# Turning four of eight score blocks off TensorE, and moving sums to GpSimd, in a fused attention and two-layer kernel

## The chip, the cores and the metric

One core of one Trainium2 chip. The metric is the device time of one execution in microseconds, as the median of repeated runs.

## The reference, cut to what matters

The kernel computes chunked attention with memory (4 batches, 8 heads, 768 positions, head size 64; chunks of 32 queries see 8 memory keys, 16 to the left, 8 to the right), then, on 3072 tokens of 512 features, a gated product layer (1536 wide), then a layer with softmax-linear units and a layer norm (1024 wide), all in float32:

```
scores = scale * q_c @ k_full.T ; a = softmax(scores) ; out = a @ v_full
x = ((x @ w_a) * (x @ w_b)) @ w_out
h = x @ w_in ; solu = h * softmax(h)
out = (layernorm(solu) * g_ln) @ w_out2
```

## The kernel before

TensorE multiplies in a reduced float format, so each operand is split in a high part (`[:, 0]`, made by ScalarE as a cast) and a low part (made by VectorE as the difference), and each product is three matmuls. The 3072 tokens are six blocks of 512. Blocks 0 and 1 go through the first layer directly (`ab`, `gate`, `x2_step`); blocks 2 to 5 go through it as two super blocks (`sb` 0 and 1) of two blocks each, with seven products instead of eight per 2x2 of submatrices. Those need sums and differences of the weights, which are made while block 1 is computed: for each of the 12 column groups q of the weights, `s1_whole` adds the high and low part back together into one half of the tile Z (half q % 2), `s1_sums` makes four sums in it, `s1_hi` casts them, `s1_lo` makes the low part in place, and both are stored to DRAM (`ws`). `wo_keep` stores the third weight and, for seven of twelve, a sum of its parts. During super block 0 `wo_load`, `wo_sums`, `wo_hi`, `wo_lo` and `wo_store` do the like for w_out in six parts p, and `piece_load` brings pieces of it into slot 8 for `third_mm`.

Attention for the later blocks is computed while the first layer of an earlier one runs. A "pair" d is two query groups of 128 queries. Pairs d0 to d0 + 3 (blocks 2 and 3) run inside block 1, pairs d0 + 4 to d0 + 7 inside super block 0. A pair has the steps `pair_P` (mask), `pair_S` (128 score matmuls), `pair_M` (maximum, subtract), `pair_X` (exponential into the tile EB), `pair_N` (sum, reciprocal, product in EB), `pair_T` (eight 128x128 transposes on TensorE into PSUM, and a copy back to EB on ScalarE), and `pair_V` (128 value matmuls, and a copy to the tile `xst`). The tiles X0 and X1 (`xst`) collect the results of blocks 2 and 3; `x1_hi`, `x1_lo` and `t1_sum` make operands of them.

The order on TensorE, VectorE, ScalarE and, from block 1 on, SyncE's DMA queue is the order in which the program is written. A clock of "ticks" lays it out: `at(t, fn, ...)` puts a step behind tick t, and `tick()` is called after each group of matmuls. Block 1 has 12 column groups f with six ticks of six matmuls each: two for the first product, two for the second (then `gate`, which multiplies and casts), two for `x2_step` of f - 1 (with `gate_lo` before its second tick). So ticks 0 to 71 are block 1, and super block 0 follows. `when(0, f, k)` gives a tick of super block 0. Loads of q, k and v for pairs go through `pair_load(d, i, values)` into three buffers in turn (`ld_tile`). GpSimd's order is not written out by hand; it makes few sums before the last stage. The pairs' places (P, S, M, X, N, T, V in ticks), the s1 steps' places and the first loads of w_out's pieces, all six ahead of super block 0:

```
pair(d0 + j, [16 * j + k for k in (-2 if j else 0, 0, 1, 2, 3, 8, 10)])
for k, fn in zip(places, (s1_whole, s1_sums, s1_hi, s1_lo)):
    at(16 * (q // 3) + k, fn, q)
for p in range(HF):
    piece_load(p)
```

Of the kernel before, what the change touches and what calls it, by code (L numbers as in the profile page):

```python
# [55 lines left out]
def fused_kernel(  # L56
# [24 lines left out]
    wos = [dram.tile([P, 4, 2, 256], F32, name=f"wos{p}") for p in range(HF)]  # L81
    ztd = [dram.tile([P // 32, P // 32, 32, NF2 * 32], F32, name=f"ztd{i}") for i in range(4)]
# [4 lines left out]
    ld_p = ctx.enter_context(tc.tile_pool(name="ld", bufs=3))  # L87

    def ld_tile(n, name):
        return ld_p.tile([P, n], F32, tag="ld", name=name, padded_shape=[P, NP * (GQ + GK)])  # L90
# [42 lines left out]

    turn = {}

    def next_of(name, n):

        turn[name] = (turn.get(name, -1) + 1) % n
        return turn[name]
# [154 lines left out]
    def pair_load(d, i, values):  # L294

        qi = 2 * d + i
        n = NP * (GQ + GK) + NCH * NP * D
        q, k = NP * GQ, NP * (GQ + GK)
        if values:
            t = ld_tile(n - k, "v")  # L300
            nc.sync.dma_start(t, qkv[qi, :, k:n])
            quads[qi]["v"] = t.rearrange("k (c p d) -> k c p d", c=NCH, p=NP)
        else:
            t = ld_tile(k, "qk")
# [33 lines left out]

    def pair_X(d):
        e = EB.rearrange("q g (p r k) -> q r (g p) k", p=NP, r=2)  # L340
        nc.scalar.activation(out=e, in_=pairs[d].pop("all"), func=AF.Exp, scale=SCALE)

    def pair_N(d):
        e = EB.rearrange("q g (h k) -> q (g h) k", h=H)
        sm = sm_p.tile([P, 2 * H, 1], F32, tag="sm2", name="sm")
        nc.vector.tensor_reduce(out=sm, in_=e, op=ALU.add, axis=AX.X)
        nc.vector.tensor_scalar_add(sm, sm, 1e-9)
        nc.vector.reciprocal(out=sm, in_=sm)
        nc.vector.tensor_tensor(
            out=e, in0=e, in1=sm.to_broadcast([P, 2 * H, CK]), op=ALU.mult  # L350
        )

    def pair_T(d):
        e = EB.rearrange("q g (p rk) -> q (g p) rk", p=NP)
        pt = ps_at.tile([P, 2 * NP, GQ], F32, tag="at", name="pt")
        for p in range(2 * NP):
            nc.tensor.transpose(pt[:, p, :], e[:, p, :], ident)
        nc.scalar.copy(EB.rearrange("q g (p t) -> q (g p) t", p=NP), pt)
# [11 lines left out]
    def pair_V1(d, i):  # L370
# [3 lines left out]
        at = EB[:, i].rearrange("q (p t) -> q p t", p=NP)  # L374
        for c in range(NCH):
            t = slice(CQ * c, CQ * c + CQ)
            for p in range(NP):
                half = 64 * (p % 2)
                for r in range(2):
# [4 lines left out]
                        at[rows, p, t],  # L384
# [4 lines left out]
    def pair_V2(d):  # L389
        pair_V1(d, 1)  # L390
        full = pairs[d].pop("px")
        bi, off = d // 2, d % 2 * 2 * GQ
        if off == 0:
            xst[bi % 2] = x_tile(bi % 2, F32, "xs")
# [100 lines left out]
    def wo_keep(f):  # L495
# [12 lines left out]
    def s1_whole(q):  # L508
# [3 lines left out]
        nc.vector.tensor_tensor(  # L512
# [63 lines left out]
    def t1_sum(n):  # L576

        a, b = stage(0), stage(1)
        if n == 0:
            xsrc.update(zip((3, 2, 6), (  # L580
                ld_tile(2 * TB, "t").rearrange("d (k t) -> d k t", k=2) for _ in range(3)
# [70 lines left out]
    def wo_sums(p):  # L652
        z = flat(wo_z(p)).rearrange("p (i c) -> p i c", i=4)
        for o, a, b, op in (
# [5 lines left out]
            nc.vector.tensor_tensor(out=z[:, o], in0=z[:, a], in1=z[:, b], op=op)  # L660
# [144 lines left out]
    def w2_raws(n):  # L805
        held.setdefault("ld", []).extend(ld_tile(2 * WC, "w2ld") for _ in range(n))
# [614 lines left out]
    def pair(d, places):  # L1421
        p, s, m, x, n, t, v = places
        for k, fn in zip(places, (pair_P, pair_S, pair_M, pair_X, pair_N, pair_T, pair_V)):
# [5 lines left out]
            if fn is pair_S:  # L1429
                at(k, pair_load, d, 1, True)  # L1430
                if d % 4 < 3:
                    at(k, pair_load, d + 1, 0, False)
            if fn in (pair_V, pair_V2) and d % 4 < 3:
                at(k, pair_load, d + 1, 1, False)
                at(k, pair_load, d + 1, 0, True)
# [498 lines left out]
```

## Time and profile before

| what | us |
|---|---|
| median of three runs | 879.94 (879.82 to 880.74) |
| the profiled execution | 880.53 |
| its span | 878.8 |
| TensorE matmul busy | 858.5 |
| VectorE busy | 718.3 |
| ScalarE busy | 398.0 |
| GpSimd busy | 63.5 |

The span is the time from the first to the last instruction of one profiled execution; the execution's own time has some 1.7 us more around it. Busy times are those of one engine's instructions without overlaps counted twice. The durations of single matmuls overlap, so the time that one takes of TensorE's queue is read from where the next begins.

### The profile page before, as it was taken

What the parts mean: (1) busy time and instruction counts of PE and PEld (TensorE: products, weight loads), DVE (VectorE), ACT (ScalarE), POOL (GpSimd) and SP (SyncE); (2) the same over time, 40 slices, a digit from 0 to 9 for tenths busy, and PEclk for the clock granted to TensorE, in tenths of its full rate; (3) what the DMA queues carried; (4) which work ended last, traced back from release to release, by engine and by line L of the source; (5) the groups of instructions that cost most, each with busy time, mean ns of one, the idle gap of its engine ahead of it and who ended that gap; (6) DMA issues with size and microseconds to landing.
All of it is one profiled execution on the core that took longest, in us unless ns stands there. A gap on an engine that the chain in (4) does not pass through costs nothing.

```text
span 878.8 us, 16702 instructions
## 1 busy us (share of the span) xinstructions
PE 858.5 (98%) x6696; PEld 709.5 (81%) x6696; DVE 718.3 (82%) x1162; ACT 398.0 (45%) x587; POOL 63.5 (7%) x77
## 2 busy tenths in 40 slices
PE   4899999999999999999999999999999999999998
PEld 3788888788888888888888888888888888888887
DVE  6999966978876676777967778998589999999892
ACT  3777633333343323334645544257354444544432
POOL 0000000000000000000000000000322222322110
PEclk9999999999999999999999999999999999999999
DMA  9995447876799878872799988558913545564344
GB/s 370 423 415 218 162 145 230 282 239 211 249 342 412 304 289 343 318 293 89 258 324 337 341 323 324 208 200 288 322 41 97 163 151 179 163 186 128 120 144 133
DMA packets 96254, 214.49 MB, mean 244 GB/s; under 512 B 7728, under 2 KB 58672, under 8 KB 90928
## 3 DMA queue, kind: packets, MB, share of 16 engines
q1 hardware_dynamic: 96144, 213.42, 68.1%
q8 instruction: 53, 0.87, 0.4%
q14 instruction: 25, 0.20, 0.1%
q0 software_dynamic: 32, 0.00, 0.0%
HBM read 147.85 MB, written 65.54 MB: 243 GB/s over the span
## 4 chain that ended last, share of the span: by engine, by line
PE 93%; DVE 3%; ACT 2%; DMA 1%; issue 1%; SPq 0%; ACTq 0%; DVEq 0%
PE acc L784 25%; PE pab L1220 15%; PE acc L998 13%; PE pab L755 7%; PE acc L755 5%; PE pab L885 5%; PE pab L886 5%; PE pab L887 5%; PE acc L885 3%; PE acc L887 2%; PE acc L886 2%; PE px L381 2%; PE s L193 2%; PE px L267 1%; DMA qkv<-qkv_dram 1%
## 5 line engine op out<-in xcount | busy, mean ns | idle before, releaser
L784 PE MATMUL acc<-w 128*128 128x512 f32 x978 | 227.6, 391 | 0.0
L784 PEld LDWEIGHTS acc<-w 128*128 128x128 f32 x978 | 182.6, 188 | 38.4 <-DMA w<-ws 0.3
L1220 PE MATMUL pab<-w 128*128 128x512 f32 (+1 forms) x600 | 134.3, 381 | 0.0
L1220 PEld LDWEIGHTS pab<-w 128*128 128x128 f32 x600 | 109.4, 188 | 21.9 <-DVE w L1197 0.3
L885 PE MATMUL pab<-x,w 128*128 128x512 f32 (+1 forms) x200 | 78.9, 394 | 1.5 <-ACT x L286 0.9
L946 POOL TENSOR_TENSOR w2ld<-w2ld 128x256 f32<-128x256 f32 x44 | 38.9, 906 | 540.5 <-ACT r L775 492.3
L886 PE MATMUL pab<-x,w 128*128 128x512 f32 (+1 forms) x200 | 77.2, 386 | 0.1
L887 PE MATMUL pab<-x,w 128*128 128x512 f32 (+1 forms) x200 | 77.1, 385 | 0.0
L755 PE MATMUL pab<-w 128*128 128x512 f32 x288 | 70.2, 390 | 0.1
L797 DVE TENSOR_TENSOR part<-acc,part 128x512 f32<-128x512 f32 x56 | 38.6, 690 | 33.3 <-PE acc L784 26.5
L755 PEld LDWEIGHTS pab<-w 128*128 128x128 f32 x288 | 53.8, 188 | 11.6 <-ACT w L726 0.5
L998 PE MATMUL acc<-w,hx 128*128 128x512 f32 x252 | 60.6, 390 | 0.1
L998 PE MATMUL acc<-w 128*128 128x512 f32 x252 | 60.3, 390 | 0.0
L998 PEld LDWEIGHTS acc<-w,hx 128*128 128x128 f32 x252 | 47.1, 188 | 10.3 <-DVE mx L1014 0.5
L998 PEld LDWEIGHTS acc<-w 128*128 128x128 f32 x252 | 47.2, 188 | 9.8
L755 PE MATMUL acc<-w 128*128 128x512 f32 x216 | 51.7, 389 | 0.0
L755 PEld LDWEIGHTS acc<-w 128*128 128x128 f32 x216 | 40.5, 188 | 8.4
L885 PEld LDWEIGHTS pab<-x,w 128*128 128x128 f32 x200 | 38.1, 191 | 9.7 <-ACT x L286 1.2
L887 PEld LDWEIGHTS pab<-x,w 128*128 128x128 f32 x200 | 38.2, 191 | 7.5
L886 PEld LDWEIGHTS pab<-x,w 128*128 128x128 f32 x200 | 38.2, 191 | 7.3 <-DVE x L290 0.4
L730 DVE TENSOR_TENSOR w<-r,w 128x512 fp32r<-128x512 f32 x56 | 37.9, 693 | 1.9 <-ACT w L726 1.9
L885 PE MATMUL acc<-gh,w 128*128 128x512 f32 x96 | 38.2, 397 | 0.0
(237 smaller groups left out, 1406.9 us busy)
## 6 DMA issues: line engine op xcount, KB each, us to landing
w<-ws SPq DMA_DIRECT2D x24, 1024.0 KB, 6.8
w<-ws SPq DMA_DIRECT2D x24, 768.0 KB, 6.0
raw<-w1d_dram SPq DMA_DIRECT2D x11, 1536.0 KB, 22.6
qk<-qkv_dram SPq DMA_DIRECT2D x20, 640.0 KB, 6.6
ws<-Z SPq DMA_DIRECT2D x24, 512.0 KB, 4.9
w<-wos SPq DMA_DIRECT2D x48, 256.0 KB, 4.1
ztd<-r SPq DMA_DIRECT2D x84, 128.0 KB, 2.3
v<-qkv_dram SPq DMA_DIRECT2D x20, 512.0 KB, 5.8
```

Source lines behind the costliest of these rows:

```text
L193: nc.tensor.matmul(s[CQ * c:CQ * c + CQ, r, p, lo:hi], st["q"][rows, p, CQ * c:CQ * c + CQ], st["k"][rows, p, k0 + lo:k0 + hi], start=True ...
L381: nc.tensor.matmul(px[half:half + 64, r, p // 2, i, t], v[rows, c, p, :], at[rows, p, t], start=True, stop=True,)
L730: nc.vector.tensor_tensor(out=c[:, 1], in0=op_src(k), in1=c[:, 0].bitcast(F32), op=ALU.subtract)
L755: nc.tensor.matmul(ps, w[:, u, sl], g[:, v], start=first and n == 0, stop=last and n == 2, skip_group_check=True,)
L784: nc.tensor.matmul(ps, w[:, u, k], xx[v][:, k], start=(start and k == 0 and i == 0), stop=(stop and k == 1 and i == 2), skip_group_check=True,
L797: nc.vector.tensor_tensor(out=o, in0=a, in1=b, op=op)
L885: nc.tensor.matmul(ps, wl, xh, start=first, stop=False)
L886: nc.tensor.matmul(ps, wh, xl, start=False, stop=False)
L887: nc.tensor.matmul(ps, wh, xh, start=False, stop=last)
L946: (nc.gpsimd if j else nc.vector).tensor_tensor(out=s4[:, i], in0=a, in1=b, op=op)
L998: nc.tensor.matmul(ps, x, y, start=(start and k == 0 and i == 0), stop=(stop and k == 1 and i == 2), skip_group_check=True,)
L1220: nc.tensor.matmul(po, s[x][:, f], wo2(f)[:, h, sl], start=(m == 0), stop=(m == 3 * NF2 - 1))
```

## The change

For pairs d0 to d0 + 3 the transposes on TensorE go. VectorE turns all of EB (128x1024) in 32x32 squares, four DMAs store it to DRAM (`etd`) so that chunk and key change places, and one DMA loads it into the columns of the X tile where the pair's result will stand later. `pair_X` and `pair_N` order EB by (r, 32-column half, head pair, column) for it, the first as two exponentials, the second with its product in two halves. The value products read the X tile. Their place moves to behind the next pair's scores, and the loads of q, k and v are put in other buffers and places for it. `s1_whole`, the sums of `wo_keep` and `wo_sums` run on GpSimd instead of VectorE, with new places for some s1 steps. The six first pieces of w_out are loaded one per f of super block 0. The core of the diff:

```diff
     def pair_T(d):
+        if not by_dma(d):
...
+            return
+        e = EB.rearrange("q r x -> q (r x)")
+        nc.vector.transpose(out=e, in_=e)
+
+    def pair_O(d):
+        m = etd[d % 2].rearrange("(i k) c x -> k i c x", i=4)
+        for c in range(NCH):
+            nc.sync.dma_start(
+                m[:, :, c], EB[CQ * c:CQ * c + CQ].rearrange("k r (b x) -> k (r b) x", b=2)
+            )
+
+    def pair_R(d):
+        bi, off = pair_xs(d)
+        at = xst[bi % 2][:, :, off:off + 2 * GQ]
+        nc.sync.dma_start(at, etd[d % 2])
+        pairs[d]["at"] = at.rearrange("k c (g p t) -> k c g p t", g=2, p=NP)
...
-                        at[rows, p, t],
+                        at[rows, c, i, p],
...
     def wo_keep(f):
...
-            nc.vector.tensor_tensor(out=t, in0=w[:, 0], in1=w[:, 1], op=ALU.add)
+            nc.gpsimd.tensor_tensor(out=t, in0=w[:, 0], in1=w[:, 1], op=ALU.add)
...
     def s1_whole(q):
...
-        nc.vector.tensor_tensor(
+        nc.gpsimd.tensor_tensor(
             out=s1[q].rearrange("p (a c) -> p a c", a=2), in0=w[:, :, 0], in1=w[:, :, 1],
...
     def wo_sums(p):
...
-            nc.vector.tensor_tensor(out=z[:, o], in0=z[:, a], in1=z[:, b], op=op)
+            nc.gpsimd.tensor_tensor(out=z[:, o], in0=z[:, a], in1=z[:, b], op=op)
...
+            if fn is pair_S and d % 4 == 0:
+                for i in range(2):
+                    at(k + 4, pair_load, d + 1, i, False, i)
+            if fn is pair_S and d % 4:
+                at(k, pair_load, d - 1, 1, True, 0)
+                at(k, pair_load, d, 0, True, d % 2 or 2)
+            if fn is pair_V:
+                if d % 4 < 2:
+                    at(k, pair_load, d + 2, 0, False, 0)
+                    at(k, pair_load, d + 2, 1, False, 1 + (d + 1) % 2)
+                if d % 4 == 2:
+                    at(k, pair_load, d + 1, 1, True, 0)
...
-        pair(d0 + j, [16 * j + k for k in (-2 if j else 0, 0, 1, 2, 3, 8, 10)])
+        pair(d0 + j, [(0, 16, 31, 46)[j] + k for k in (
+            (-2 if j else 0, 0, 1, 2, 4 - (j > 0), 6 - (j > 0) - (j > 2), 7 - 2 * (j > 2), 10 - (j > 2), 17 if j > 2 else 23)
+        )])
...
-        places = ((1, 3, 6, 8), (8, 9, 11, 13), (14, 15, 17, 20))[q % 3]
-        if q == 6:
-            places = 1, 3, 8, 9
+        places = ((0, 3, 6, 8), (7, 9, 11, 13), (13, 15, 17, 20))[q % 3]
+        if q < 4:
+            places = ((2, 7, 8, 10), (9, 11, 14, 16), (14, 17, 19, 20), (1, 5, 7, 8))[q]
...
-        at((0, 0, 14, 14, 14, 32, 32, 44, 48, 52, 56, 60)[f], wo_keep, f)
+        at((0, 0, 18, 19, 20, 34, 35, 44, 48, 52, 56, 60)[f], wo_keep, f)
...
+        at(when(0, p + 1, 1), piece_load, p)
         at(when(1, p, 2), piece_load, p)
...
-    for p in range(HF):
-        piece_load(p)
```

So pair j has its scores behind tick 0, 16, 31 and 46, its turn behind tick 6, 21, 36 and 50, its stores behind 7, 23, 38 and 51, its load behind 10, 26, 41 and 55, and its values behind 23, 39, 54 and 63.

## Rows read from the trace of the kernel before

**Rows 1.** The page: span, busy time of TensorE and VectorE.

```profile
span 878.8 us, 16702 instructions
...
PE   858.5 (98%) x6696; PEld 709.5 (81%) x6696; DVE 718.3 (82%) x1162; ACT 398.0 (45%) x587; POOL 63.5 (7%) x77
```

**Rows 2.** Windows: stretch, length, busy us of each engine, granted clock, DMA share, GB/s.

```profile
147.00:262.00 115.00, 113.86 (x1478) 94.60 (x1479) 95.30 (x136) 42.52 (x54) 0.00 (x0) 0.99 0.77 260
262.00:410.00 148.00, 148.00 (x1624) 121.95 (x1623) 101.61 (x149) 51.92 (x77) 0.00 (x0) 1.00 0.79 299
...
147.00:150.00 3.00, 2.96 (x122) 2.74 (x126) 1.51 (x3) 0.00 (x0) 0.00 (x0) 0.50 0.56 175
```

**Rows 3.** TensorE's timeline: start, us, what, [idle before, releaser]; first and second pair.

```profile
157.74 1.06 PE L357 MATMUL pt<-ident,EB 128*128 128x128 f32 x8 [0.82 <-DVE EB L349]
...
161.84 2.07 PE L381 MATMUL px<-EB,v 64*64 64x32 f32 x128 [0.28 <-ACT EB L358]
...
172.24 1.54 PE L193 MATMUL s<-qk 64*32 64x64 f32 x128
...
184.50 0.39 PE L887 MATMUL pab<-x,w 128*128 128x512 f32 x1
184.74 1.03 PE L357 MATMUL pt<-ident,EB 128*128 128x128 f32 x8
185.53 0.48 PE L885 MATMUL pab<-x,w 128*128 128x512 f32 x1
185.84 0.40 PE L886 MATMUL pab<-x,w 128*128 128x512 f32 x1
```

**Rows 4.** The chain that ended last: one run of 36 matmuls.

```profile
430.84 8.16 PE acc L755 x36
```

**Rows 5.** VectorE's groups by line, 147 to 262 us: busy us, mean ns.

```profile
L526 DVE TENSOR_TENSOR Z<-Z 128x256 f32<-128x256 f32 x48 | 20.4, 424 | 1.3
L543 DVE TENSOR_TENSOR Z<-Z 128x1024 fp32r<-128x1024 f32 x12 | 14.7, 1222 | 3.3 <-ACT Z L536 3.3
L512 DVE TENSOR_TENSOR Z<-w 128x1024 f32<-128x1024 f32 x12 | 14.6, 1217 | 1.9 <-DMA ws<-Z 1.9
...
L900 DVE TENSOR_TENSOR G<-G,pab 128x512 f32<-128x512 f32 x12 | 8.2, 684 | 7.6 <-PE pab L887 7.6
...
L349 DVE TENSOR_TENSOR EB<-EB,sm 128x1024 f32<-128x1024 f32 x4 | 4.9, 1226 | 0.1
...
L503 DVE TENSOR_TENSOR wz<-w 128x512 f32<-128x512 f32 x7 | 4.5, 684 | 0.0
```

**Rows 6.** Groups by line, whole span: GpSimd's sums, wo_sums, VectorE's 32x32 turn.

```profile
L946 POOL TENSOR_TENSOR w2ld<-w2ld 128x256 f32<-128x256 f32 x44 | 38.9, 906 | 540.5 <-ACT r L775 492.3 <-DVE w L975 28.0 <-DVE hx L975 19.4
...
L1169 DVE STREAM_TRANSPOSE r<-r 128x1024 f32<-128x1024 f32 x13 | 16.2, 1244 | 0.2
...
L660 DVE TENSOR_TENSOR r<-r 128x256 f32<-128x256 f32 x24 | 10.2, 424 | 0.6
...
L225 POOL TENSOR_TENSOR EB<-EB,sm 128x512 f32<-128x512 f32 x2 | 2.1, 1044 | 121.9 <-DVE sm L224 121.9
```

**Rows 7.** DMA issues, 147 to 262 us: KB each, median us to landing.

```profile
ws<-Z SPq DMA_DIRECT2D x24, 512.0 KB, 4.9
qk<-qkv_dram SPq DMA_DIRECT2D x6, 640.0 KB, 6.2
v<-qkv_dram SPq DMA_DIRECT2D x7, 512.0 KB, 5.6
```

**Rows 8.** DMA issues of the page, whole span: the last stage's stores.

```profile
ztd<-r SPq DMA_DIRECT2D x84, 128.0 KB, 2.3
```

**Rows 9.** Timelines of VectorE and GpSimd, 660 to 700 us: one meeting.

```profile
691.92 1.72 DVE L1106 TENSOR_TENSOR r<-r,EB 128x1024 f32<-128x1024 f32 x1
...
688.50 4.06 POOL L946 TENSOR_TENSOR w2ld<-w2ld 128x256 f32<-128x256 f32 x4 [4.64 <-DVE hx L975]
```

More of the change, by code (lines that the diff above doesn't have):

```diff
@@ L81, in fused_kernel @@
     wos = [dram.tile([P, 4, 2, 256], F32, name=f"wos{p}") for p in range(HF)]
+    etd = [dram.tile([P, NCH, 8 * CQ], F32, name=f"etd{i}") for i in range(2)]
     ztd = [dram.tile([P // 32, P // 32, 32, NF2 * 32], F32, name=f"ztd{i}") for i in range(4)]
@@ L337, in pair_M, with by_dma @@
         )
+    def by_dma(d):
+        return d < 4 * NDIR
     def pair_X(d):
-        e = EB.rearrange("q g (p r k) -> q r (g p) k", p=NP, r=2)
-        nc.scalar.activation(out=e, in_=pairs[d].pop("all"), func=AF.Exp, scale=SCALE)
-    def pair_N(d):
-        e = EB.rearrange("q g (h k) -> q (g h) k", h=H)
-        sm = sm_p.tile([P, 2 * H, 1], F32, tag="sm2", name="sm")
-        nc.vector.tensor_reduce(out=sm, in_=e, op=ALU.add, axis=AX.X)
+        if not by_dma(d):
+            e = EB.rearrange("q g (p r k) -> q r (g p) k", p=NP, r=2)
+            nc.scalar.activation(out=e, in_=pairs[d].pop("all"), func=AF.Exp, scale=SCALE)
+            return
+        e = EB.rearrange("q r (b n k) -> q r n b k", b=2, n=2 * NP)
+        s = pairs[d].pop("all").rearrange("q r n (b k) -> q r n b k", b=2)
+        for r in range(2):
+            nc.scalar.activation(out=e[:, r], in_=s[:, r], func=AF.Exp, scale=SCALE)
@@ L347, in pair_N @@
         nc.vector.tensor_scalar_add(sm, sm, 1e-9)
         nc.vector.reciprocal(out=sm, in_=sm)
-        nc.vector.tensor_tensor(
-            out=e, in0=e, in1=sm.to_broadcast([P, 2 * H, CK]), op=ALU.mult
-        )
-    def pair_T(d):
[L354 to L358, printed above, removed]
+        for r in range(2):
+            nc.vector.tensor_tensor(
+                out=EB[:, r].rearrange("q (b n k) -> q b n k", b=2, n=2 * NP),
+                in0=EB[:, r].rearrange("q (b n k) -> q b n k", b=2, n=2 * NP),
+                in1=sm[:, r].rearrange("q (b n k) -> q b n k", b=1, k=1).to_broadcast(
+                    [P, 2, 2 * NP, 32]),
+                op=ALU.mult,
+            )
@@ new lines, in pair_T @@
+    def pair_T(d):
+        if not by_dma(d):
+            e = EB.rearrange("q g (p rk) -> q (g p) rk", p=NP)
+            pt = ps_at.tile([P, 2 * NP, GQ], F32, tag="at", name="pt")
+            for p in range(2 * NP):
+                nc.tensor.transpose(pt[:, p, :], e[:, p, :], ident)
+            nc.scalar.copy(EB.rearrange("q g (p t) -> q (g p) t", p=NP), pt)
+            pairs[d]["at"] = EB.rearrange("q g (p c t) -> q c g p t", p=NP, c=NCH)
+            return
+        e = EB.rearrange("q r x -> q (r x)")
+        nc.vector.transpose(out=e, in_=e)
@@ L580, in t1_sum @@
             xsrc.update(zip((3, 2, 6), (
[L581 removed]
+                ld_tile(2 * TB, "t", i).rearrange("d (k t) -> d k t", k=2) for i in range(3)
             )))
@@ L805, in w2_raws @@
     def w2_raws(n):
-        held.setdefault("ld", []).extend(ld_tile(2 * WC, "w2ld") for _ in range(n))
+        t = held.setdefault("ld", [])
+        t += [ld_tile(2 * WC, "w2ld", len(t) + i) for i in range(n)]
     def w2_z(i):
@@ L1508, in fused_kernel @@
     )):
-        pair(d0 + 4 + j, [when(0, f, k) for f, k in places])
-    for t, *n in ((74, 0, False), (74, 1, False), (78, 0, True)):
+        places = [when(0, f, k) for f, k in places]
+        pair(d0 + 4 + j, [*places[:6], None, None, places[6]])
+    for t, *n in ((74, 0, False, 0), (74, 1, False, 1), (78, 0, True, 2)):
         at(t, pair_load, d0 + 4, *n)
```

75 lines of the change are left out of this document (49 added, 26 removed).

## The prediction, made before the run

> **What bounds the kernel now.** I read the page's busy shares first: TensorE is busy 858.5 of 878.8 us, VectorE 718.3 [rows 1]. So TensorE's queue is the kernel, and an edit gains only if it takes instructions or idle time out of that queue. Next the windows by stage. The edits lie in the second block (147 to 262 us) and the first super block after it (262 to 410). TensorE is busy 113.86 of 115 us in the one and all 148 in the other [rows 2]. In the first window 1.14 us of idle time is thus all that could be recovered besides work; in the second nothing. VectorE is busy 95.3 of the 115 us and 101.6 of the 148: heavily loaded, but not what TensorE waits for, since TensorE does not stop.
>
> The reader should then find the idle time in TensorE's timeline. Before the first pair's eight transposes it waits 0.82 us for VectorE's normalised EB, and before that pair's value products 0.28 us for ScalarE's copy of the turned EB [rows 3]. That is 1.10 of the 1.14 us. The second pair's transposes begin with no wait, and so do the third's and fourth's.
>
> **The change part by part.**
>
> *Transposes leave TensorE.* In the timeline a matmul starts at 184.50, the eight transposes at 184.74, the next matmul at 185.53 and the one after at 185.84 [rows 3]. A matmul normally takes 8.16/36 = 0.227 us of the queue [rows 4]. So the eight cost 185.53 - 184.50 - 0.227 = 0.80 us, and the restart 0.31 - 0.227 = 0.08 more: 0.88 us. Four pairs: **3.5 us**. Nothing replaces them on TensorE: scores and value products keep their number and shapes, the value products read 32 contiguous columns as before, only from the X tile instead of EB.
>
> *The two waits.* With values at tick 23 after scores at tick 0, neither the normalisation nor a copy of EB stands before a TensorE instruction: **1.1 us**. If the wait merely moves, this term is 0.
>
> *VectorE.* A 32x32 turn of 128x1024 takes 1.245 us [rows 6], the normalising product in two halves some 0.2 more than its 1.23 [rows 5] (an estimate from the fixed part that 424 ns for 256 columns against 1222 for 1024 imply). Four pairs add 5.7 us. The twelve s1_whole (14.6) and seven wo_keep sums (4.5) leave it [rows 5], in the next stage the 24 wo_sums (10.2) [rows 6]. Net it falls from 95.3 to about 82 us in the block and from 101.6 to 91 behind it. TensorE has no use for that: worth 0. ScalarE loses a copy per pair and splits an exponential, on an engine busy 42.5 of 115 us [rows 2]: 0.
>
> *The way through DRAM.* Four stores of 128 KB per pair; the nearest row is ztd<-r, the same size, 2.3 us to landing [rows 8]. One load of 512 KB; the nearest row is v, 5.6 us [rows 7]. A tick is six matmuls, 1.36 us [rows 4]. Pair 0: store at tick 7, load at 10, values at 23: 13 ticks or 17.7 us for 5.6. The shortest is pair 3: load at 55, values at 63: 10.9 us. Cost 0 while these margins stand. The load waits on SyncE's queue for the stores to land, and everything later on that queue (Z stores, loads of the next q, k and v) waits with it, for at most the 2.3 us.
>
> *Loads of q, k and v change places.* Pair 3's two q,k loads are issued after pair 1's values (tick 39), its scores follow tick 46: 7 ticks, 9.5 us, for two loads of 6.2 us median that start 0.5 us apart and share the DMA engines [rows 7]. I take 7.5 us, so 2 us in hand. Pair 2 has 8 ticks. The DMA share is 0.77 in this stretch [rows 2] and the new way adds 4 MB to its 115 us x 260 GB/s = 30 MB, so there is room on average.
>
> *Sums on GpSimd.* The trace shows 128x512 at 1044 ns and 128x256 at 906 ns on GpSimd [rows 6]. An s1_whole (128x1024) lies between twice the first, 2.1 us, and four times the second, 3.6 us; I take 2.1, its runs of 512 being nearest to the first. It frees VectorE and is due only at s1_sums. The loop for one half of Z is whole 2.1 to 3.6, sums 4 x 0.424 = 1.7, cast and lo 1.2 each [rows 5] (the cast taken as long as lo), store 4.9 [rows 7]: 11.1 to 12.6 us. Two q's have 32/3 ticks, 14.5 us, plus the inserted scores and values. It fits.
>
> The tightest place is q = 10. Count from the start of pair 3's scores. VectorE then has M 2.4, sums(8) 1.7, x1_lo 1.2, N 3.1, turn 1.2, gate 0.7, sums(9) 1.7, gate_lo 0.7, lo(8) 1.2 [rows 5, 6], after 1.54 us of scores [rows 3]: lo(8) ends at 15.4. Its store lands at 20.3, GpSimd ends at 22.4 to 23.9, sums(10) and gate_lo(9) at 24.8 to 26.3. TensorE wants gate_lo(9) behind tick 63, at 17 x 1.36 + 1.54 + 2 x 2.07 = 28.8. So 2.5 to 4 us in hand: cost 0.
>
> There is a row against free overlap of the two engines: a soft_mult of 128x1024 takes 1.72 us where VectorE's other sums and products of that size take 1.22 [rows 5], and it begins at 691.92 while GpSimd runs its h_sums from 688.50 to 692.56 [rows 9]. So a collision costs VectorE about 0.5 us. The Trainium skill, "SBUF — State Buffer", Who interferes with whom, says that a VectorE instruction with two SBUF inputs and a GpSimd instruction reading SBUF lock each other out until the first has finished; the trace agrees with that row. By it each of the 19 sums of this block could hold VectorE for its whole 1.0 to 2.1 us rather than 0.5; at the worst VectorE would get no relief, and the sum above would still be -4.6 us, as TensorE doesn't wait for it.
>
> By the row, 19 collisions are at most 9.5 us of VectorE, half of the 19.1 it is rid of.
>
> *wo_sums and wo's pieces.* Each wo_sums becomes 4 x 906 = 3.6 us instead of 1.7, but GpSimd starts when the load lands: wo_load comes 9 or more ticks (12 us) before its sums' old place. ScalarE's wo_hi, two ticks behind that place, finds them done: 0. The six pieces, loaded one per f and used some 12 ticks later, are as hidden as they were: 0.
>
> **Sum.** 3.5 + 1.1 = 4.6 us. The profiled execution took 880.53 us (its span 878.8 and 1.7 around it), so 875.9 for one like it; the median of the runs is 0.59 below that execution, so **875.3 us**.
>
> **Rivals.**
>
> 1. *A late transfer takes a share.* For it: the margin of 2 us at pair 3's scores, and SyncE's queue now stands behind the turn (store) and behind the store (load). Against: q,k loads with only 4.5 ticks behind the values stop TensorE nowhere now. If pair 2's and 3's loads take 9.5 to 11 us instead of 7.5, each stop costs up to 1.5 us, and a load of pair 3's turned weights another 1: 1 to 4 us, so 876.3 to 879.3.
>
> 2. *VectorE, held by GpSimd, makes TensorE wait: slower.* VectorE's order is fixed, so a late GpSimd sum holds gate_lo behind it, and TensorE's x2 step wants that. It decides from the point where VectorE is over 2.5 to 4 us late at tick 64. Eight collisions of 0.5 us before it, or a store landing at 9 instead of 4.9 us, bring it there. At q = 7, 9 and 10, 2 to 3 us each are 6 to 9 us lost: 877 to 884, taken as 882. Against: the block has net 13 us less for VectorE.
>
> 3. *The wait moves, the work goes.* Only the 3.5 us are won, the 1.1 us come back elsewhere (the first wait for pair 0's turned weights cannot, at 17.7 us): 876.4.
>
> 4. *A bonus.* From 147 to 150 us TensorE has a granted clock of 0.50, its 1.2 GHz level [rows 2], after a stretch of small products and waits at the end of the first block. Those 3 us cost 1.5. The change touches nothing in front of them, but the loads and VectorE's first sums there move; if the fall were gone: 873.8.
>
> **How the numbers follow.** The forecast has 0.58, rival 1 0.16, rival 2 0.10, rival 3 0.11, rival 4 0.05. Forecast's own range: 3.2 (restarts not counted) to 1.14 + 3.6 = 4.7 us, with the runs' own 0.9 us of spread: 874.6 to 876.7. The range of 873.8 to 878.3 leaves out rival 2 and the upper third of rival 1, and the rest is some 8 in 10. A measurement of this kernel can tell about 0.2%, 1.76 us, from no change. Faster: forecast, 3, 4 and two thirds of 1, 0.84, less a little for what I haven't seen: 0.81. Same: the rest of 1 and part of 2: 0.10. Slower: 0.09.
>
> **What the profile after would show.** No transposes out of EB for four of the eight pairs; TensorE's busy time and span down by 3.5 or more; no idle before the first pair's values; the lines of pair_T on VectorE at about 1.25 us, x4; s1_whole on GpSimd at 2.1 us (3.6 would be the other bound); VectorE's waits for GpSimd new, under 3 us each; TensorE's idle time in the second block under 0.3 us. The prediction is wrong if TensorE waits for q,k loads before the third or fourth pair's scores, for X before the values, or for gh or gl at an x2 step.

## The result, and the profile after

The changed kernel takes **890.32 us** (median of four runs, 889.19 to 890.66); the kernel before, run beside it, 880.15 (879.82 to 880.74). The ratio is 1.0113 [1.0095, 1.013]: slower by 1.1%, where 0.5% faster was forecast. One execution of the runs below, the profiled one of loads_first2 (1431.6 us at a granted clock of 0.56 throughout), is in no median and no comparison.

The page after, with the lines that answer to [rows 1]:

```profile
span 888.3 us, 16721 instructions
...
PE 858.1 (97%) x6664; PEld 708.2 (80%) x6664; DVE 705.8 (79%) x1127; ACT 393.5 (44%) x587; POOL 122.8 (14%) x120
```

32 transposes have left TensorE, as the change says. Its busy time is still nearly what it was, and the span is 9.5 us longer: idle time has come in, and TensorE spends more of its time at the lower clock, where a matmul of 512 columns is busy for 0.63 us and not 0.39. The windows after, to be set against [rows 2]; the last two are stretches at the lower clock, 10.2 us in all, where the kernel before has one of 3.4, from 146.95 (the execution's last 1.4 us not counted; busy us of TensorE, its weight loads, VectorE, ScalarE, GpSimd; granted clock, DMA share, GB/s):

```profile
147.00:262.00 115.00, 108.93 (x1491) 90.17 (x1492) 82.96 (x122) 36.52 (x53) 29.62 (x13) 0.96 0.83 273
262.00:410.00 148.00, 145.42 (x1609) 119.04 (x1608) 92.72 (x121) 51.03 (x74) 19.54 (x24) 1.00 0.84 314
...
147.27:154.08 6.81, 5.61 (x180) 4.70 (x183) 0.97 (x3) 1.23 (x3) 0.00 (x0) 0.50 0.39 115
225.78:229.17 3.39, 2.95 (x68) 2.44 (x69) 1.69 (x2) 0.00 (x0) 1.43 (x1) 0.50 1.09 386
```

VectorE has the relief that was worked out (95.3 to 83.0 us in the second block), and TensorE stands still 6.1 of 115 us in place of 1.1. TensorE's timeline names the places; for landmarks it holds the first matmul of the scores of pairs d0, d0 + 4 and d0 + 7:

```profile
142.66 1.14 PE L270 MATMUL px<-AT,v 64*64 64x32 f32 x64
146.88 0.79 PE L238 MATMUL pt<-ident,EB 128*128 128x128 f32 x4 [3.08 <-DVE EB L228]
...
152.63 1.94 PE L196 MATMUL s<-qk 64*32 64x64 f32 x128
...
196.76 1.47 PE L196 MATMUL s<-qk 64*32 64x48 f32 x128 [0.59 <-PE pab L944]
...
224.76 0.85 PE L196 MATMUL s<-qk 64*32 64x64 f32 x64 [3.67 <-DMA qk<-qkv_dram]
226.22 1.19 PE L196 MATMUL s<-qk 64*32 64x64 f32 x64 [0.61 <-DMA qk<-qkv_dram]
...
280.79 1.47 PE L196 MATMUL s<-qk 64*32 64x64 f32 x128
...
284.36 0.96 PE L840 MATMUL acc<-w 128*128 128x512 f32 x3 [1.67 <-issue]
...
380.10 0.32 PE L439 MATMUL px<-EB,v 64*64 64x32 f32 x7 [0.80 <-issue]
...
387.37 1.47 PE L196 MATMUL s<-qk 64*32 64x64 f32 x128
```

The same landmarks before, in its own timeline:

```profile
148.40 2.05 PE L193 MATMUL s<-qk 64*32 64x64 f32 x128
...
275.08 1.47 PE L193 MATMUL s<-qk 64*32 64x64 f32 x128
...
378.38 1.47 PE L193 MATMUL s<-qk 64*32 64x64 f32 x128
```

The reader is to see four things. TensorE is 4.2 us late at the first pair's scores (152.63 against 148.40), before the changed block has begun. It is 5.7 us late at 280.79, 9.0 at 387.37 and 9.5 at the end. None of the idle time of [rows 3] is left. And three of the new stops are not where the prediction looked: the end of the first block, and two stops with no releaser (the waits of an engine that no semaphore in the trace ends; `issue` in the rows). Worked out over the rows: 4.2 to the first landmark; in the second block 0.59 + 3.67 + 0.61 of waits and half of the 3.4 us at 1.2 GHz behind them, 1.7, less the 4.6 that the change takes out, is 2.0 (the landmarks say 1.5); then 1.67 and 0.80. Some 1.3 us to the end I have not placed, but for a gap of 0.29 at 600 us.

### The profile page after: what moved, and what is told of

Same layout as the page of the kernel before. It is cut to its first block, busy times and chain, and to the rows that moved or that the text cites. A ratio compares the mean times of both kernels' runs of the same rounds, so it can differ in the third digit from the quotient of the medians.

```text
span 888.3 us, 16721 instructions
## 1 busy us (share of the span) xinstructions
PE 858.1 (97%) x6664; PEld 708.2 (80%) x6664; DVE 705.8 (79%) x1127; ACT 393.5 (44%) x587; POOL 122.8 (14%) x120
## 4 chain that ended last, share of the span: by engine, by line
PE 86%; DMA 5%; DVE 4%; ACT 2%; issue 2%; SPq 1%; POOL 0%; ACTq 0%; POOLq 0%
PE acc L840 25%; PE pab L1277 13%; PE acc L1055 12%; PE pab L811 7%; PE acc L811 5%; PE pab L942 4%; PE pab L943 4%; PE pab L944 4%; PE acc L942 2%; PE acc L944 2%; PE acc L943 2%; DMA ws<-Z 2%; PE s L196 1%; PE px L270 1%; PE px L439 1%
## 5 line engine op out<-in xcount | busy, mean ns | idle before, releaser
L1055 PEld LDWEIGHTS acc<-w,hx 128*128 128x128 f32 x252 | 47.2, 188 | 10.2 <-DVE mx L1071 0.5
L568 POOL TENSOR_TENSOR Z<-w 128x1024 f32<-128x1024 f32 x12 | 30.5, 2542 | 76.9 <-DMA ws<-Z 65.2
```

Source lines behind the costliest of these rows:

```text
L568: nc.gpsimd.tensor_tensor(out=s1[q].rearrange("p (a c) -> p a c", a=2), in0=w[:, :, 0], in1=w[:, :, 1], op=ALU.add,)
L1055: nc.tensor.matmul(ps, x, y, start=(start and k == 0 and i == 0), stop=(stop and k == 1 and i == 2), skip_group_check=True,)
```

## The experiments

The expectations give their theories letters. **A**: the sums on GpSimd cost the time, first of all where s1_whole of q = 0 and 1 meets VectorE at the end of the first block. **A2** (A in loads_first, F in final1 and final2): SyncE's order costs it, as loads of q, k stand behind stores; against it **B2**: the DMA engines are full there, so that an earlier issue lands no earlier. **B** and **E**: the way through DRAM as a whole is the cause. **C**: the stops with no releaser depend on where instructions lie in TensorE's program, not on what they do. **D**: the loop of store, GpSimd's sum and VectorE's sums over the halves of Z makes VectorE late. "Pair 2" and "pair 3" in them are pairs d0 + 2 and d0 + 3, the third and fourth here. The medians in one table; the kernel before, run beside them, had 880.2 to 880.7:

| run | us | ratio to before [95%] |
|---|---|---|
| sums_vec | 894.66 | 1.0167 [1.015, 1.0184] |
| gp_only | 887.56 | 1.0079 [1.0062, 1.0096] |
| early_vec | 888.45 | 1.0096 [1.0081, 1.0111] |
| gp_early_vec | 883.84 | 1.0039 [1.0025, 1.0052] |
| loads_first | 898.46 | 1.0204 [1.0182, 1.0225] |
| loads_first2 | 892.22 | 1.0148 [1.0119, 1.0176] |
| both | 892.8 | 1.014 [1.0119, 1.016] |
| both_pad | 891.42 | 1.0127 [1.0105, 1.015] |
| loads_act | 890.84 | 1.0134 [1.0111, 1.0156] |
| no_dram | 887.04 | 1.0079 [1.0064, 1.0094] |
| pad_only | 889.7 | 1.0102 [1.0084, 1.012] |
| all3 | 891.09 | 1.012 [1.0105, 1.0135] |
| z3 | 890.83 | 1.012 [1.0096, 1.0145] |
| z3_early_pad | 886.63 | 1.0066 [1.0048, 1.0084] |
| final1 | 888.54 | 1.0109 [1.0088, 1.0131] |
| final2 | 889.5 | 1.0112 [1.0096, 1.0128] |

### GpSimd's sums alone, and the turn alone

sums_vec: the changed kernel with all three sums back on VectorE.

```diff
-            nc.gpsimd.tensor_tensor(out=t, in0=w[:, 0], in1=w[:, 1], op=ALU.add)
+            nc.vector.tensor_tensor(out=t, in0=w[:, 0], in1=w[:, 1], op=ALU.add)
...
-        nc.gpsimd.tensor_tensor(
+        nc.vector.tensor_tensor(
...
-            nc.gpsimd.tensor_tensor(out=z[:, o], in0=z[:, a], in1=z[:, b], op=op)
+            nc.vector.tensor_tensor(out=z[:, o], in0=z[:, a], in1=z[:, b], op=op)
```

> The changed kernel with all three kinds of sums (s1_whole, wo_keep's sums, wo_sums) back on VectorE at the changed places; the turn through DRAM stays. Theory A (GpSimd's sums run free of the ticks: two s1_whole at 141.6 us hold VectorE up before the last transposes of the first block, 3.1 us of TensorE idle and 3.4 us more at 1.2 GHz, and later VectorE waits for them, so that pair 3's q and k are loaded late, 4.3 us of idle and another 3.4 us at 1.2 GHz): the first loss goes (-4.8 us), the second goes or shrinks: 879.5 to 883 us, no idle over 0.5 us before the transposes at 141 us. Rival B (the way through DRAM on SyncE's queue is the cause, GpSimd is not): 888 or more, the wait for q and k at pair 3's scores stays at 4 us.

gp_only: the kernel before with the three sums on GpSimd, and nothing else of the change.

```diff
-            nc.vector.tensor_tensor(out=t, in0=w[:, 0], in1=w[:, 1], op=ALU.add)
+            nc.gpsimd.tensor_tensor(out=t, in0=w[:, 0], in1=w[:, 1], op=ALU.add)
...
```

s1_whole and wo_sums are changed in the same way.

> The kernel before with the three kinds of sums on GpSimd at the places of before, nothing else changed. Theory A: the first loss comes alone, some 3 us idle before the last transposes of the first block and 1.7 us of slow clock, so 884 to 886 us; the pairs' turns by TensorE stay, and VectorE's waits for s1_whole may add 1 to 3 us to it through a late EB. Rival B: 879 to 881 us, as before.

The two parts, the turn with its moved loads and places and the sums, cost 14.3 and 7.2 us by themselves and 10.2 together, so each is a loss, and the sums on GpSimd buy back some of what the turn costs. For sums_vec theory A missed: the stop at 147 is gone, but VectorE, now with the turn on top of all its sums, makes TensorE wait at other places. TensorE's timeline of sums_vec:

```profile
187.33 0.50 PE L942 MATMUL pab<-x,w 128*128 128x512 f32 x1 [3.08 <-DVE G L957]
...
222.79 0.50 PE L943 MATMUL acc<-gh,w 128*128 128x512 f32 x1 [1.22 <-DVE gh L963]
...
228.09 1.17 PE L196 MATMUL s<-qk 64*32 64x64 f32 x64 [3.87 <-ACT gh L959]
```

For gp_only theory A held in its mechanism, though 887.56 us is above its 884 to 886: with no turn, no stores and no moved load, the stop at the end of the first block is there with nearly the same size. TensorE's timeline of gp_only:

```profile
145.63 1.11 PE L235 MATMUL pt<-ident,EB 128*128 128x128 f32 x4 [2.89 <-DVE EB L225]
```

### The meeting at the end of the first block

GpSimd's timeline of the changed kernel, and VectorE's for the same stretch:

```profile
130.56 5.46 POOL L559 TENSOR_TENSOR wz<-w 128x512 f32<-128x512 f32 x4 [3.84 <-PE pab L943]
141.60 4.67 POOL L568 TENSOR_TENSOR Z<-w 128x1024 f32<-128x1024 f32 x2 [5.58 <-ACT EB L217]
```

```profile
138.41 0.17 DVE L226 TENSOR_SCALAR sm<-sm 128x8 f32<-128x8 f32 x1
...
138.86 0.69 DVE L228 TENSOR_TENSOR EB<-EB,sm 128x512 f32<-128x512 f32 x1
...
142.35 1.66 DVE L226 TENSOR_SCALAR sm<-sm 128x8 f32<-128x8 f32 x1
...
144.28 2.55 DVE L228 TENSOR_TENSOR EB<-EB,sm 128x512 f32<-128x512 f32 x1
```

GpSimd has the block's first sums in its queue with nothing ahead of them, and starts when their data are free, at 130 and 141 us; the program has them behind tick 0 and later, and the six matmuls of tick 0 begin at 150.81. VectorE's two last steps of the first block, alone 0.17 and 0.69 us a few us before, take 1.66 and 2.55 beside it, and TensorE's last transposes of that block wait for them. The two additions on GpSimd end at 143.98 and 146.27; the first of the two steps ends at 144.0, the second at 146.8, as if each had waited for the addition beside it. early_vec takes only this meeting away.

```diff
-        nc.gpsimd.tensor_tensor(
+        (nc.vector if q < 2 else nc.gpsimd).tensor_tensor(
```

> The changed kernel with the s1_whole of q = 0 and 1 alone back on VectorE, at their ticks. Theory A: the 3.1 us idle before the transposes of the first block's last queries go, and the slow clock there is as short as before (3.4 us): 890.3 - 4.8 = 885.5 us; pair 3's wait for q and k stays, about 4 us. If the idle time there has another cause: 890.

VectorE's and TensorE's timelines of early_vec:

```profile
141.80 0.69 DVE L228 TENSOR_TENSOR EB<-EB,sm 128x512 f32<-128x512 f32 x1
```

```profile
145.80 0.38 PE L942 MATMUL pab<-x,w 128*128 128x256 f32 x1 [0.48 <-ACT x L289]
...
219.89 1.17 PE L196 MATMUL s<-qk 64*32 64x64 f32 x64 [3.07 <-DMA qk<-qkv_dram]
```

The first matmul behind that block stands at 145.80, in the changed kernel at 150.81: 5.0 us won there, 3.08 of the wait and 1.9 at 1.2 GHz. The time falls by 1.9 only. What is lost again stands in the same timeline: waits of 1.66 before the third pair's scores (0.59 in the changed kernel), 3.07 + 0.60 before the fourth's (3.67 + 0.61), 1.63 and 1.27 with no releaser (1.67 and 0.80), and stretches of 6.8 and 3.4 us at 1.2 GHz behind them, for one of 3.4. In six profiles of kernels that keep the meeting TensorE waits 1.1 to 3.1 us there. In that of loads_act GpSimd starts at 142.80, when VectorE is done with these steps, and it costs nothing; so a microsecond decides it.

gp_early_vec is the same edit on gp_only: no turn, and no early meeting.

> The kernel before with the sums on GpSimd, except the s1_whole of q = 0 and 1: what GpSimd's sums cost without the meeting at the end of the first block. Theory A2: 887.6 - 2.9 (idle) - 3.4 (6.8 us less at 1.2 GHz) = 881.3, of which 1 to 2 are VectorE's later EB; if GpSimd's sums cost elsewhere too: over 883.

It is the best of the runs with sums on GpSimd, and still 3.2 us over before (ten runs from 880.86 to 886.12). GpSimd's other sums thus cost about 3 us by themselves; where, its profile does not show, since that execution was one of the shortest (881.37). It is not the clock: the six executions at a mean granted clock of 1.000 spread from 880.9 to 884.9.

### SyncE's order before the fourth pair's scores

SyncE's timeline of the changed kernel (start, us to issue), and two rows of its DMA issues: q, k issued from 218.0 to 218.5 us, and the load of pair d0 + 2's turned weights (KB, us to landing):

```profile
214.34 0.37 SPq L587 DMA_DIRECT2D ws<-Z  x1
214.75 2.71 SPq L401 DMA_DIRECT2D etd<-EB  x4
...
218.05 1.68 SPq L310 DMA_DIRECT2D qk<-qkv_dram  x2
```

```profile
qk<-qkv_dram SPq DMA_DIRECT2D x1, 640.0 KB, 6.6
...
xs<-etd SPq DMA_DIRECT2D x1, 512.0 KB, 8.5
```

The values of pair d0 + 1 end at 211.3 (209.26 + 2.07), and from then on the loads could go. They go at 218.05 and behind it, 6.7 us later: a store of Z stands ahead of them and waits for VectorE's low part, and four stores behind it take 2.71 us to issue. That low part stands in VectorE's order behind the sums of q = 6 and the turn, and part of its lateness is a wait for GpSimd, whose half of Z waits for a store to land. GpSimd's and VectorE's timelines show it for q = 5:

```profile
197.62 3.14 POOL L568 TENSOR_TENSOR Z<-w 128x1024 f32<-128x1024 f32 x1 [5.91 <-DMA ws<-Z]
```

```profile
200.80 1.80 DVE L582 TENSOR_TENSOR Z<-Z 128x256 f32<-128x256 f32 x4 [2.29 <-POOL Z L568]
...
213.09 1.18 DVE L599 TENSOR_TENSOR Z<-Z 128x1024 fp32r<-128x1024 f32 x1
```

This wait is not all of it: z3 below takes it out, and the loads go only 0.5 us earlier.

Two kernels put the loads ahead of the stores. loads_first moves pair d0 + 2's stores behind its tick 39, and q = 5's last step with them; in it, q = 5's low part is made from a buffer that already holds q = 6's high part.

```diff
-    7 - 2 * (j > 2), 10 - (j > 2)
+    7 + (j == 2) - 2 * (j > 2), 10 - (j > 2)
...
+        if q == 5:
+            places = 13, 15, 17, 23
```

> The changed kernel with two places moved: pair 2's four stores behind the loads of pair 3's q and k on SyncE's queue (tick 39 instead of 38), and q = 5's low part with its store behind them too (tick 39 instead of 36). Theory A: the loads are issued some 6 us earlier, right behind pair 1's values, pair 3's scores wait under 0.5 us and the slow clock behind them is gone: 890.3 - 4.3 - 1.7 = 884.3 us. If the loads were slow because the DMA engines are full, not because they were issued late: 888 to 890, and the loads take over 8 us to land.

loads_first2 moves only the DMAs; in it, q = 5's low part is stored after q = 7's first sum has overwritten that half of Z, and so too in both and both_pad.

```diff
-        s1_store(q, 0, h)
+        if q == 6:
+            at(39, s1_store, q, 0, h)
+        else:
+            s1_store(q, 0, h)
```

The same is done for the low part of q = 5, with loads_first's place of the stores.

> The changed kernel with the order on SyncE's queue changed around tick 39 alone: pair 3's q and k are loaded ahead of pair 2's four stores to DRAM and of two stores of weight sums (q = 5 low, q = 6 high); every engine computes in the order of the changed kernel. Theory A2 (these loads were late because they stood behind stores that waited for a late VectorE): they are issued right behind pair 1's values, some 6 us earlier, and the 4.3 us of idle time before pair 3's scores go with their 3.4 us at 1.2 GHz (1.7 us): 884 to 885 us. Rival B2 (the DMA engines are full there, so issuing earlier doesn't land them earlier): the idle time stays over 2 us, 887 to 890.

Both lost more than they won: 8 and 2 us over the changed kernel. In loads_first the wait before the fourth scores is gone, and 6.00 us for VectorE's gate and 4.04 for the next load of turned weights stand in its place. Its trace shows why: the stores of Z now stand behind the loads, GpSimd waits 18.4 us for one to land before its next sum, and VectorE 10.6 us for that sum. As the moved steps also change what waits for what, neither kernel tests the order alone. There is no trace of loads_first2 to compare; both, which adds early_vec's edit to it, shows the same in TensorE's timeline:

> That order on SyncE's queue, and the s1_whole of q = 0 and 1 on VectorE. Theory A2: the two losses are separate places and add: 890.3 - 5.0 - 6.0 = 879.3 us, with idle time left only where nothing in the profile is waited for (some 3 us in all). If one loss merely moves: 883 or more.

```profile
241.09 0.50 PE L948 MATMUL pab<-x,w 128*128 128x512 f32 x1 [2.81 <-DVE G L963]
...
254.86 2.25 PE L439 MATMUL px<-xs,v 64*64 64x32 f32 x128 [2.60 <-DMA xs<-etd]
```

loads_act issues these loads from ScalarE's queue instead, so that nothing of SyncE's stands ahead:

```diff
-                    at(k, pair_load, d + 2, 0, False, 0)
-                    at(k, pair_load, d + 2, 1, False, 1 + (d + 1) % 2)
+                    at(k, pair_load, d + 2, 0, False, 0, nc.scalar)
+                    at(k, pair_load, d + 2, 1, False, 1 + (d + 1) % 2, nc.scalar)
```

> The changed kernel with the q,k loads of pairs 2 and 3 issued from ScalarE's queue, behind its copy of the values, instead of SyncE's; nothing else moves. Theory A2 (the loads were late because they stood behind stores on SyncE's queue): pair 3's loads are issued within 2 us of the end of pair 1's values instead of 6.8 us, and the 4.3 us idle before pair 3's scores go with 3.4 us at 1.2 GHz: 884 to 885 us. Rival B2 (the DMA engines are full): the idle time stays over 2 us and it is 887 to 890.

ScalarE's timeline of loads_act, and TensorE's:

```profile
208.89 1.05 ACT L592 CAST Z<-Z 128x1024 fp32r<-128x1024 f32 x1 [5.71 <-DVE Z L599]
209.61 0.34 ACTq L310 DMA_DIRECT2D qk<-qkv_dram  x1
...
212.45 0.33 ACTq L310 DMA_DIRECT2D qk<-qkv_dram  x1
```

```profile
219.98 1.18 PE L196 MATMUL s<-qk 64*32 64x64 f32 x64 [3.04 <-DMA qk<-qkv_dram]
...
251.52 1.73 PE L439 MATMUL px<-xs,v 64*64 64x32 f32 x101 [2.62 <-DMA xs<-etd]
```

Here the first load waits behind ScalarE's cast of Z, which waits 5.71 us for VectorE, and the second comes 2.84 us behind the first, 6.0 us after the values end (206.41). The first half of the scores is in time; the second half waits for the second load. The lateness that reaches TensorE through SyncE's order reaches it through ScalarE's too.

no_dram takes the way through DRAM out: a copy on ScalarE stands in place of the four stores and the load, so that the weights stand in the wrong squares and that part of the computation is left out.

```diff
-        for c in range(NCH):
+        for c in range(0):
...
-        nc.sync.dma_start(at, etd[d % 2])
+        nc.scalar.copy(at, EB.rearrange("q r (b x) -> q (r b) x", b=2))
```

> The changed kernel without the way through DRAM: VectorE turns EB, and ScalarE copies it to the X tile in place of the four stores and the load, so the weights stand in the wrong squares (this part of the computation is left out). Theory D: the loop over Z stays, so VectorE's waits for GpSimd between 170 and 206 us stay at 2 us or more; pair 3's loads, without 2.7 us of stores ahead of them, wait 1.5 to 3 us instead of 4.3: 887 to 889. Rival E: all idle time but that at 145 us and the instruction fetches' goes: 882 to 884.

Without it the loads of q, k go at 213.59, 3.5 us behind the values where the changed kernel has 6.7, and the fourth scores wait 0.73 us in place of 4.28. The meeting (2.90 us) and the stops with no releaser (1.10, 1.46) are still there. The way through DRAM thus has some 3 to 4 us of the 10.2 (890.3 against 887.0, or 10.2 against 6.4 over the kernel before beside each); the rest is of other causes.

Taken together, the traces say what sets this wait. The second of the two loads takes 7.0 to 7.6 us to land in the changed kernel, early_vec, pad_only, z3, z3_early_pad, both, final1, final2 and no_dram, with or without the turn's DMAs. Where the loads are issued 6.0 to 6.8 us after the values end (the first five), the fourth scores wait 3.3 to 4.3 us; at 3.1 to 4.1 us (final2, no_dram, final1) they wait 0.2 to 1.0; at 1.0 (both) not at all. So it is the place on the queue (A2), and not full DMA engines (B2).

### The stops with no releaser

At 284.36 and 380.10 TensorE waits for nothing that semaphores show. The DMA view of the changed kernel does show something: in a window of 0.1 us from 281.90, 2.4 us ahead of the first matmul behind the stop, the one packet of the queue for instructions between 277 and 284.5 (packets, MB, share):

```profile
q8 instruction: 1, 0.02, 63.7%
```

On the page that queue has 52 packets and 0.85 MB, so 16 KB each, and TensorE has 6664 matmuls and as many weight loads: some 256 instructions a packet. At 380.10 the packet starts 2.4 us ahead as well. 128 small matmuls with their weight loads are one packet's worth and run in 1.5 to 2.1 us; a stretch of 128 large ones takes 29. pad_only tries this: 32 matmuls of 32x32 at the start of the changed kernel, so that everything behind lies later by a part of a packet.

```diff
+    def pad(n):
+        t = ps_ab.tile([P, TB], F32, tag="ps0", name="pad")
+        for _ in range(n):
+            nc.tensor.matmul(t[0:32, 0:32], ident[:, 0:32], ident[:, 0:32], start=True, stop=True)
+
     att_P(0)
+    pad(16)
     att_S(0)
+    pad(16)
```

> The changed kernel with 32 small matmuls (64 instructions, as many as the transposes taken out) added on TensorE among the first scores, where it waits for loads. Theory C (the idle times with no releaser, 1.67 us at 284 us and 0.80 us at 380 us, come from where the instruction fetches fall): both go, 887 to 888.5 us, and the idle times with a releaser stay. Rival: both stay, 890.

both_pad is both with the same addition.

> As the last, with 32 small matmuls on TensorE put before the first scores, where it is idle anyway. Theory C (the idle times with no releaser, 1.6 us at 280 us and 1.3 us at 378 us, come from where the boundaries of TensorE's instruction fetches fall; the 64 transpose instructions that the change takes out moved them): the 64 added instructions move them back, these two idle times go and it is 2 to 3 us faster than the last. Rival: they come from a DMA or an engine at that place, and stay.

Both texts count 64 added instructions. pad_only's page shows twice that, 64 matmuls and 64 weight loads more than the changed kernel has (x6664 each), so half a packet:

```profile
PE 861.5 (97%) x6728; PEld 711.2 (80%) x6728; DVE 707.1 (80%) x1127; ACT 393.6 (44%) x587; POOL 123.1 (14%) x120
```

Both stops are gone in every kernel that has the addition and there in each profile of a kernel with the turn and without the addition. TensorE's timeline of pad_only at the place, and near the start, where a new stop has come:

```profile
25.80 1.59 PE L270 MATMUL px<-EB,qkv 64*64 64x32 f32 x49 [1.69 <-issue]
...
279.99 1.47 PE L196 MATMUL s<-qk 64*32 64x64 f32 x128
281.38 6.87 PE L840 MATMUL acc<-w 128*128 128x512 f32 x29
```

Theory C holds, and a count settles it. If all of TensorE's records are numbered in order, matmuls, weight loads and waits, then 706, 6338 and 8386 records stand ahead of the stops of the changed kernel at 21.61, 284.36 and 380.10 us, and 705 and 962 ahead of those of pad_only at 19.36 and 25.80: each 193 or 194 above a multiple of 256. The same holds for every stop over 0.25 us without a releaser in 17 profiles (all but loads_first2's), but for two before the third pair's scores (early_vec, all3).

The time moved by 0.6 us only, within the spread (both_pad against both: 1.4). Two stops of 2.5 us in all went; near the start, one of 2.24 became one of 1.26, and one of 1.69 came. The addition also delays the first block: its last value products begin at 145.8 to 146.8 us in the five profiles that have it and not the meeting, at 144.2 to 145.3 in the six that have neither.

### What remains when the fixes are put together

all3 has early_vec's, loads_act's and pad_only's edits.

> The three together: q = 0 and 1 of s1_whole on VectorE, the q,k loads of pairs 2 and 3 from ScalarE's queue, the 32 small matmuls. Theory A2 with C: 890.3 - 5.0 - 6.0 - 2.5 = 877 us, under the kernel before, with under 3 us of idle time from 140 us to 600 us. If the losses move to other waits as VectorE stays as loaded as it is: 880 to 885.

It is no faster than the changed kernel. The stops at the end of the first block and at 280 and 380 us are gone; the third pair's scores wait 1.07 us, the fourth's 1.93, a matmul 2.88 for VectorE's gate, and the last pair's values 1.08 for the turned weights.

z3 gives q = 0 to 5 a third buffer, out of the upper half of X1, so that GpSimd need not wait for a store to land.

```diff
+        if q < 6:
+            s1[q] = (Z[:, 0:2 * WC], Z[:, 2 * WC:4 * WC], flat(s1["wz"][:, 2:4]))[q % 3]
...
-            t = s1["wz"][:, f % 4]
+            t = (s1["wz"][:, 0], s1["wz"][:, 1], AT)[f % 3]
```

> The changed kernel with a third buffer for the sums of q = 0 to 5 (the upper half of X1, which wo_keep's sums leave for AT), so that GpSimd's s1_whole of q = 2 to 5 needn't wait for the store of q - 2. Theory D (the loop of store, GpSimd's sum and VectorE's sums over two halves of Z is longer than TensorE's 17 us for two q's, so VectorE falls some 5 us behind by pair 2, and the loads of pair 3 behind it on SyncE's queue): VectorE's waits for GpSimd between 170 and 206 us (3.7 us) go, pair 3's q and k are issued 3 to 5 us earlier and its scores wait under 1.5 us: 885 to 887 us. Rival E (the traffic of the turn through DRAM fills the queue, the loop does not matter): 889 to 891, the idle time before pair 3's scores stays at 3 us or more.

VectorE's waits for GpSimd between 170 and 206 us (3.7 in the changed kernel) are gone, but the loads of q, k still go 6.2 us after the values, for 6.7, and the fourth scores wait 2.57 + 1.00 us. So theory D missed: without the loop's waits the loads are hardly earlier. GpSimd, no longer held, meets VectorE elsewhere. VectorE's and GpSimd's timelines of z3; the step of L601 takes 1.22 us alone:

```profile
194.86 3.22 DVE L601 TENSOR_TENSOR Z<-Z 128x1024 fp32r<-128x1024 f32 x1
```

```profile
194.62 2.37 POOL L570 TENSOR_TENSOR Z<-w 128x1024 f32<-128x1024 f32 x1 [6.47 <-DVE gh L965]
```

z3_early_pad adds early_vec's and pad_only's edits to z3.

> The same with the s1_whole of q = 0 and 1 on VectorE and with the 32 small matmuls. Theory D: 877 to 880 us, as three separate losses are gone (4 to 6, 5 and 2.5 us). If VectorE's and SyncE's load is the limit: 883 to 888, with idle time at new places.

It is the best with the turn, 3.7 us under the changed kernel, but the fourth scores still wait 2.65 + 0.65 us. final1 and final2 put the stores of pair d0 + 2 behind tick 39, and steps of q = 6 (final1) or of q = 5 and 6 (final2) later.

```diff
+        if q == 5:
+            places = 13, 18, 20, 22
+        if q == 6:
+            places = 0, 5, 7, 9
```

Those are final2's; final1 has only q = 6, at 0, 3, 7, 8.

> z3_early_pad with pair 2's four stores at tick 39 behind pair 3's q,k loads, and the cast of q = 6 with its store at tick 39 instead of 38, behind them too. Theory F (order on SyncE's queue, the four stores' 2.7 us above all): the loads are issued 2 to 3.4 us earlier, pair 3's scores wait under 1 us and no 1.2 GHz stretch follows: 886.6 - 3 - 3.4 = 880 to 882 us. If VectorE's lateness alone sets it: 885 or more and a wait over 2 us.

> The same with VectorE's sums of q = 5 and 6 three and two ticks later, so that pair 2's maximum, product and turn no longer stand behind them. Theory F: the turn and the low part of q = 5 end 2 to 4 us earlier, no wait for q and k at pair 3's scores: 878 to 881 us; under 880.7 would beat the kernel before. If GpSimd's sums just meet other VectorE instructions: as the last, 880 to 886.

In final1 the fourth scores wait 0.98 us, and TensorE waits 1.52 and 1.81 us for VectorE's gate steps and 2.70 for the last pair's turned weights. In final2 the fourth scores wait 0.18 us, as wanted, and TensorE waits 2.65 us for v instead:

```profile
236.07 1.93 PE L439 MATMUL px<-xs,v 64*64 64x32 f32 x64 [2.65 <-DMA v<-qkv_dram]
```

Nothing tried beats the kernel before.

## Why the prediction was wrong

- **Transposes and the two waits, 3.5 + 1.1 us: right as far as the trace shows.** The 32 transposes and the idle time of [rows 3] are gone, and nothing stands before a pair's values for VectorE or ScalarE; with 4.6 us taken off, the sum over the second block comes to 2.0 where the landmarks show 1.5. The wait did not move in that form, so rival 3 fell.
- **The turn on VectorE: right.** It takes 1.24 us (1.245 forecast). VectorE's 83.0 us in the block fit the forecast of 82.
- **The sums' size: right; their start: the first step that failed.** s1_whole takes 2.39 us undisturbed and 2.54 in the mean, inside the bounds of 2.1 and 3.6 (2.1 was taken). But the prediction costed when each was due, and not when GpSimd would begin: it has no other work, and runs ahead of the ticks. The meeting at the end of the first block, at a place that the diff does not touch, made TensorE 4.2 us late at the first landmark (early_vec wins 5.0 there).
- **A collision "costs VectorE about 0.5 us": mis-sized.** It cost 1.5 (0.17 to 1.66) and 1.9 (0.69 to 2.55) here, and 2.0 in z3. The one row it came from [rows 9] was a meeting with four short additions of 0.9 us; these are single additions of 2.3. The Trainium skill, "SBUF — State Buffer", Who interferes with whom, says that the one blocks the other for a whole instruction; the measured 1.9 and 2.0 lie below one addition of 2.3 to 2.4, and the held steps end just behind it; that fits, and 0.5 does not. The prediction weighed it, and dismissed it as TensorE doesn't wait for VectorE; in the first block it does.
- **The loop over one half of Z, 11.1 to 12.6 us: mis-sized.** The forecast added its steps back to back. From q = 5's s1_whole at 197.62 to q = 7's at 217.99 it took 20.4 us: 3.2 for the sum, 1.8 for the four sums, then 10.5 for other steps that stand in VectorE's order, 1.2 for the low part and 3.7 for the store. VectorE waits 11.9 us in all for GpSimd (seven times, each under 3 us, as forecast). What this cost TensorE by itself is not shown; z3, which takes the loop's waits out up to 206 us, is no faster.
- **"2 us in hand, cost 0" at the fourth pair's scores: the second step that failed.** The forecast let the loads go when pair d0 + 1's values end. They went 6.7 us later, for what stands ahead of them on SyncE's queue; of the queue the prediction counted landings (2.3 us), not the wait of a store for a late VectorE nor the 2.7 us to issue four stores. The landings, 6.6 and 7.6 us, are what the forecast took (7.5). It cost 4.28 us and 1.7 at 1.2 GHz, and it is the prediction's own sign of being wrong. This is rival 1 at its place, above its 1 to 4 us, though by a late issue and not by slow transfers.
- **Rival 2's mechanism was at work, at another place.** GpSimd did hold VectorE, and TensorE did wait for it, but at the end of the first block. At tick 64, where rival 2 put it, TensorE does not wait.
- **Stops with no releaser, 2.5 us: not foreseen**, though the trace of before has one of 2.11 us near its start that could have been a warning. Taking out 32 transposes with their weight loads, 64 instructions, and moving the values has shifted what lies at the ends of the 256-instruction pieces.
- **The clock.** Rival 4's gain occurs in early_vec and gp_early_vec: no stretch at 1.2 GHz at the end of the first block. It does not follow from the edit alone, as both has early_vec's edit and a stretch of 3.4 us there. In the changed kernel TensorE stops for 3.08 us, and the stretch at 1.2 GHz behind it is 6.8 us long, where the kernel before has one of 3.4.

What stays open: why the single fixes don't add up (each late step is waited for by others, and the runs show the wait in another place each time, but no run follows one microsecond all the way); the 0.59 us before the third scores; the 1.3 us towards the end that are not placed; what the moved places of the s1 steps and of the pieces of w_out cost, which no run changes alone; and where GpSimd's sums cost their last 3 us in gp_early_vec.

## What to carry to other kernels

An engine with an empty queue starts its work as soon as data allow, so a step that is moved to an idle engine is costed at its earliest start as well as at its due time, and against whatever the other engine does then. Before a load is called free, write down what stands ahead of it on its queue, what each of these waits for, and how long they take to issue: here 2.7 us for four small stores and a wait for VectorE cost more than the landing had in hand. In this kernel, where four engines and the DMAs are all within a microsecond or two of being waited for, each edit that took one wait away left TensorE waiting at other places.

## What the hardware showed unexpectedly

TensorE can stop for its own program. In 17 profiled executions of the kernels, before and after among them, every stop of TensorE over 0.25 us without a releaser, but for two before the third pair's scores, ends 2.2 to 2.7 us after a 16 KB packet of the instruction queue starts, at the same place in a count of 256 instructions, and 128 instructions at the start move such stops elsewhere. The Trainium skill, "Runtime: NRT & Kernel Launch", Instruction fetch mechanics, says that instructions come in blocks of 16 KiB (256 instructions) and that crossing from one to the next is mostly hidden; the packets agree, and at 3 of 52 crossings of the changed kernel it was not hidden, for 2.24, 1.67 and 0.80 us; the first of them is in the kernel before too, with 2.11.

A GpSimd addition also held a VectorE step with one tiny operand: the addition of a constant to 128x8 values took 1.66 us in place of 0.17. And a load of one size lands in very different times: the turned weights, 512 KB, took 4.6, 4.1, 8.5 and 6.9 us for the four pairs. The DMA share from issue to landing is 1.0 in all four, so the share alone does not tell them apart; why is not shown.
